# Moving one VectorE step of a unit function by half an item in 18 items, and 27 sums from GpSimd to VectorE

## The chip, the cores and the metric

The kernel runs on one core of a Trainium2 chip, in one launch. The metric is the device time of that launch in microseconds; several runs are given by their median. TensorE (PE) does the matmuls into PSUM, VectorE (DVE), ScalarE (ACT) and GpSimd (POOL) the element-wise work, and SyncE (SP) issues nearly all transfers. Each engine works its instructions off in the order in which they stand in its queue.

## What is computed

Three layers in a row, in float32. Only their core matters here:

```python
# 1: linear attention with decay, 4 batches x 8 heads, 768 steps of 48
state = alpha[:, :, t, :, None] * state + np.einsum('bhd,bhe->bhde', k[:, :, t], v[:, :, t])
y[:, :, t] = np.einsum('bhd,bhde->bhe', q[:, :, t], state)
# 2: x is 3072 x 384 from here on; w_in 384 x 2048, w_out 2048 x 384
h = x @ w_in
g = np.where(h > 0.0, h, alpha * (np.exp(np.minimum(h, 0.0)) - 1.0))
x = g @ w_out
# 3: four experts of 1024 hidden units, weighed by normalised probabilities
for e in range(E):
    h = np.maximum(x @ w1[e], 0.0)
    out += p[:, e:e + 1] * (h @ w2[e])
```

## The kernel before

The 3072 tokens are worked in six chunks of 512 (128 positions of four batches). To keep float32 accuracy with fast matmuls, each operand is split into a high part (a ScalarE copy with rounding, "cast") and a low part (a subtraction, `value - high`), and each product is three matmuls: high by high, high by low, low by high.

**Attention** (units of 128 positions of one batch, four to a chunk). A unit's steps are `scores` (two PSUM banks a, L252), `ktrans` (transposes of k into a bank h, L273), `prep0` to `prep2` for the next unit (running products P on VectorE, L207; Ln and Exp on ScalarE, L215 to L217; products nt, raw on VectorE, L230 to L242, the last of them q times P), `yout_t` and `state` (L309, L316, L343), the masked scores sm (VectorE, L260), the copy yt (ScalarE, L324), a way out to memory and back into another layout (x0d, then xr), and `xtrans`, which splits xr into the second layer's x (L377, L378). After `state`, VectorE adds tmp and st (L353, L355). The first chunk's units run ahead of the main loop.

**Second layer.** The main loop of `run` goes over 96 items. An item is one block f of 128 hidden units of one chunk c. The order is chunk 0 with f = 0 to 7, chunk 1 with all 16, chunk 0 with f = 8 to 15, then chunks 2 to 5. In item i TensorE runs `first` (nine matmuls h = w x, L425, into one of three banks h0 to h2, which the transposes of `ktrans` use in turn with them) and `second` of item i - 2 (nine matmuls t += w g, L450). Between them the unit function and its split are made:

- `elu(h)`: ScalarE e = relu(-h) (L434), e = exp(-e) (L435), then VectorE h = max(e - 1, h) in place in PSUM (L436);
- `parts(h)`: ScalarE g high = copy of h (L441) at once; VectorE g low = h - g high (L442), returned as `low` and run later.

In the loop, `self.queue` holds deferred steps; `flush` runs them, twice an item; `slots` holds the attention steps of the next chunk and the weights' conversions by half item; `post` holds steps at an item's end. The first FS = 8 items split h right after `elu`; the others at the item's end, with the low part first in the next flush. Weights of the second layer come as 64-bit words in a buffer ring of two (wraw, L394) and are converted by ScalarE (cv, L408) and three VectorE steps on bits (L78, L81, L84), then split (w_W, L377, L378). The conversions f = 3 to 15 lie in items 0 to 15. When a part of a chunk ends, three ScalarE copies x1raw (L963) empty the banks t.

**Third layer.** From the end of the second layer on, three blocks at a time are multiplied by a scheme that needs sums of x blocks: for the first pair of chunks `prep_x0` makes 12 sums xs (`sum_x`, L567) and splits 15 blocks into tiles xc (`split`), spread over the items 81 to 94, beside the preparation of the third layer's weights (`prep_w`, tiles wc and wh). Before, the sums and the low parts of xc are on GpSimd.

What sets the order: TensorE, ScalarE, VectorE and GpSimd run in the order in which the code is written (`manual_schedule`). Only the transfers on SyncE are placed by a scheduler, which may put them in another order when the code moves.

## Time and profile before

| what | value |
|---|---|
| median of three runs | 1289.72 us (1289.24 to 1292.94) |
| profiled execution | 1294.53 us, span 1292.7 us |
| mean granted clock of TensorE | 0.985 of full speed |
| second layer with the rest of the attention | about 39 to 552 us |
| third layer | about 552 us to the end |

The profile lists, for each instruction or group, its start, its duration and, in brackets, how long its engine stood idle before it and which engine, tile and line ended that wait. L numbers are lines of the kernel before; in the changed kernel lines from 66 on are one higher, and those behind L436 move with the edits. The rows that are used stand in a section below.

### The profile page before, as it was taken

What the parts mean: (1) busy time and instruction counts of PE and PEld (TensorE: products, weight loads), DVE (VectorE), ACT (ScalarE), POOL (GpSimd) and SP (SyncE); (2) the same over time, 40 slices, a digit from 0 to 9 for tenths busy, and PEclk for the clock granted to TensorE, in tenths of its full rate; (3) what the DMA queues carried; (4) which work ended last, traced back from release to release, by engine and by line L of the source; (5) the groups of instructions that cost most, each with busy time, mean ns of one, the idle gap of its engine ahead of it and who ended that gap; (6) DMA issues with size and microseconds to landing.
All of it is one profiled execution on the core that took longest, in us unless ns stands there. A gap on an engine that the chain in (4) does not pass through costs nothing.

```text
span 1292.7 us, 17676 instructions
## 1 busy us (share of the span) xinstructions
PE 1248.4 (97%) x6453; PEld 1015.9 (79%) x6457; DVE 892.4 (69%) x1513; ACT 588.2 (46%) x1076; POOL 522.2 (40%) x405
## 2 busy tenths in 40 slices
PE   8687999999999999999999999999999999999997
PEld 6566788788888888778888888788888878888886
DVE  8976766787777867766757666666667576657664
ACT  5555655566666656633334341434333233233241
POOL 0000000000000004738679774777779475456562
PEclk8789999999999999999999999999999999999999
DMA  6543325566565647744646468755555775435232
GB/s 227 196 159 114 106 64 170 187 241 221 209 220 183 238 166 250 264 183 158 235 145 231 176 233 338 249 216 195 204 191 203 266 291 183 173 106 204 98 114 72
DMA packets 71823, 248.28 MB, mean 192 GB/s; under 512 B 6712, under 2 KB 38296, under 8 KB 62384
## 3 DMA queue, kind: packets, MB, share of 16 engines
q1 hardware_dynamic: 70720, 241.56, 52.6%
q10 hardware_dynamic: 1008, 5.51, 1.1%
q8 instruction: 53, 0.87, 0.3%
q14 instruction: 42, 0.34, 0.1%
HBM read 182.89 MB, written 64.14 MB: 191 GB/s over the span
## 4 chain that ended last, share of the span: by engine, by line
PE 82%; DVE 7%; ACT 4%; DMA 3%; issue 2%; POOL 1%; SPq 0%; ACTq 0%; DVEq 0%; POOLq 0%
PE h L729 24%; PE t L776 14%; PE t L450 12%; PE h L425 11%; PE a L776 10%; PE h L776 5%; PE a L252 2%; PE a L309 1%; PE a L316 1%; DMA wraw<-in_wm_dram 1%; PE h L273 1%; DMA xr<-x0d 1%; DVE cv L81 1%; DVE h L436 1%; DVE wh L378 1%
## 5 line engine op out<-in xcount | busy, mean ns | idle before, releaser
L749 DVE TENSOR_TENSOR u<-h,u 128x512 f32<-128x512 f32 x258 | 177.6, 688 | 87.4 <-PE h L729 86.4
L707 POOL TENSOR_TENSOR g_W<-c,g_W 128x512 fp32r<-128x512 f32 x128 | 164.6, 1301 | 156.4 <-ACT c L705 127.7
L450 PE MATMUL t<-g,w_W 128*128 128x512 f32 x864 | 218.9, 397 | 8.1 <-ACT x1raw L963 3.3
L729 PE MATMUL h<-xc_Q,wa 128*128 128x512 f32 x780 | 218.8, 390 | 2.8 <-DVE c L749 2.2
L425 PE MATMUL h<-x,w_W 128*128 128x512 f32 x864 | 216.9, 395 | 3.4 <-ACT x L377 2.8
L567 POOL TENSOR_TENSOR xs<-xr 128x512 f32<-128x512 f32 x8 | 12.4, 1568 | 494.5 <-DVE wc L478 494.5
L704 ACT ACTIVATE g_W<-c 128x512 fp32r<-128x512 f32 x128 | 80.2, 627 | 265.9 <-DVE c L749 149.5
L450 PEld LDWEIGHTS t<-g,w_W 128*128 128x128 f32 x864 | 162.1, 190 | 45.9 <-DVE g L442 5.6
L425 PEld LDWEIGHTS h<-x,w_W 128*128 128x128 f32 x864 | 161.8, 189 | 39.2 <-ACT x L377 3.6
L729 PEld LDWEIGHTS h<-xc_Q,wa 128*128 128x128 f32 x780 | 145.9, 188 | 35.0 <-DVE c L749 2.6
L776 PE MATMUL t<-g_W,wb 128*128 128x512 f32 x576 | 157.6, 389 | 0.0
L436 DVE SCALAR_TENSOR_TENSOR h<-e,h 128x512 f32<-128x512 f32 x96 | 66.6, 694 | 97.4 <-ACT e L435 97.1
L776 PEld LDWEIGHTS t<-g_W,wb 128*128 128x128 f32 x576 | 108.1, 188 | 22.5
L705 ACT ACTIVATE c<-c 128x512 f32<-128x512 f32 x192 | 121.4, 633 | 7.5 <-POOL g_X L707 0.4
L749 DVE TENSOR_TENSOR c<-u,h 128x512 f32<-128x512 f32 x123 | 84.1, 686 | 46.4 <-PE h L729 42.0
L743 DVE COPY u<-h 128x512 f32<-128x512 f32 x99 | 67.9, 690 | 64.1 <-PE h L729 63.8
L729 PE MATMUL h<-xc_W,wa 128*128 128x512 f32 x390 | 110.0, 391 | 0.8 <-DVE c L749 0.7
L707 POOL TENSOR_TENSOR g_X<-c,g_X 128x512 fp32r<-128x512 f32 x64 | 82.0, 1298 | 67.9 <-ACT c L705 64.5
L776 PE MATMUL a<-g_W,wb 128*128 128x512 f32 x384 | 108.4, 389 | 0.0
L704 ACT ACTIVATE g_X<-c 128x512 fp32r<-128x512 f32 x64 | 40.1, 626 | 131.4 <-DVE c L749 73.3
L729 PEld LDWEIGHTS h<-xc_W,wa 128*128 128x128 f32 x390 | 72.8, 188 | 17.7 <-DVE c L749 1.6
L442 DVE TENSOR_TENSOR g<-h,g 128x512 fp32r<-128x512 f32 x96 | 65.8, 685 | 27.4 <-ACT g L441 27.2
(139 smaller groups left out, 1943.1 us busy)
## 6 DMA issues: line engine op xcount, KB each, us to landing
wa<-wad SPq DMA_DIRECT2D x33, 1536.0 KB, 6.5
wb<-wbd SPq DMA_DIRECT2D x30, 1536.0 KB, 7.2
raw<-in_att_dram SPq DMA_DIRECT2D x22, 960.0 KB, 4.9
wad<-wh SPq DMA_DIRECT2D x44, 384.0 KB, 2.7
wbd<-wh SPq DMA_DIRECT2D x43, 384.0 KB, 4.4
xcd<-xh SPq DMA_DIRECT2D x30, 512.0 KB, 3.2
wraw<-in_wm_dram SPq DMA_DIRECT2D x16, 768.0 KB, 4.4
wraw<-in_we_dram SPq DMA_DIRECT2D x20, 576.0 KB, 4.7
```

What stands on the lines that cost most here:

```text
L252: nc.tensor.matmul(ps[j][:, a * C:(a + 1) * C], raw[r, K0 + a * C:K0 + (a + 1) * C], raw[r, Q0 + a * C:Q0 + (a + 1) * C], start=True, stop ...
L425: nc.tensor.matmul(h[:, 0:n], w[:, wl, fi, k * 128:(k + 1) * 128], x[:, xl, k, n0:n0 + n], start=(k == 0 and i == 0), stop=(k == KD - 1 an ...
L436: nc.vector.scalar_tensor_tensor(out=h, in0=e, scalar=-1.0, in1=h, op0=ALU.add, op1=ALU.max)
L442: return g, lambda: nc.vector.tensor_tensor(out=g[:, 1], in0=h, in1=g[:, 0].bitcast(F32), op=ALU.subtract)
L450: nc.tensor.matmul(self.xa[k][:, 0:n], w[:, wl, fi, DM + k * 128:DM + (k + 1) * 128], g[:, gl, 0:n], start=(first and i == 0), stop=(last ...
L704: nc.scalar.activation(out=g[:, n, 0], in_=v, func=AF.Relu)
L705: nc.scalar.activation(out=v, in_=v, func=AF.Relu)
L707: lambda: nc.gpsimd.tensor_tensor(out=g[:, n, 1], in0=v, in1=g[:, n, 0].bitcast(F32), op=ALU.subtract)
L729: nc.tensor.matmul(b, w[:, wl], x[:, xl], start=(j == 0), stop=(j == 2))
L743: nc.vector.tensor_copy(out, b)
L749: (nc.vector if "b" in (a0, a1) or dst == "S5" else nc.gpsimd).tensor_tensor(out=out, in0=val(a0, b), in1=val(a1, b), op=ALU.add if op == ...
L776: nc.tensor.matmul(oa[m, d], wt[:, f, wl, d * 128:(d + 1) * 128], G[m][:, f, gl], start=first, stop=last)
```

## The change

A constant WIDE = 18 is added. `elu` no longer issues its VectorE step but returns it. For items 0 to 17 that step (L436) is issued at the item's end, behind the second flush, `second`, the half item's slots and `post`; the high copy of g (L441) follows in the next item behind its `first`, and the low part (L442) behind that item's first flush and first slots. From item 18 on the order is what it was. In `prep_x0` the sums and the low parts name VectorE and no longer GpSimd.

```diff
--- before.py
+++ after.py
@@ -63,6 +63,7 @@
 )
 ORDER = [p for p, _ in STEPS]
 WSLOT = {p: i for i, p in enumerate((7, 11, 1, 6, 4, 2, 13, 12, 10, 3, 8, 14, 0, 9, 5))}
+WIDE = 18
 WPREP = (28, 92)
 
 
@@ -433,7 +434,7 @@
         e = self.ep.tile([128, 512], F32, tag="e", name="e")
         nc.scalar.activation(out=e, in_=h, func=AF.Relu, scale=-1.0)
         nc.scalar.activation(out=e, in_=e, func=AF.Exp, scale=-1.0)
-        nc.vector.scalar_tensor_tensor(out=h, in0=e, scalar=-1.0, in1=h, op0=ALU.add, op1=ALU.max)
+        return lambda: nc.vector.scalar_tensor_tensor(out=h, in0=e, scalar=-1.0, in1=h, op0=ALU.add, op1=ALU.max)
 
     def parts(self, h):
         nc = self.nc
@@ -586,13 +587,13 @@
 
         def base(p):
             s[p] = tmp[:, len(s)]
-            self.sum_x(nc.gpsimd, s[p], p, x, s)
+            self.sum_x(nc.vector, s[p], p, x, s)
 
         def summ(p):
             if p not in s and len(XSUM[p]) > 1:
                 v[p] = tmp[:, 2 + sn[0] % 4]
                 sn[0] += 1
-                self.sum_x(nc.gpsimd, v[p], p, x, s)
+                self.sum_x(nc.vector, v[p], p, x, s)
 
         def one(p):
             i = ORDER.index(p)
@@ -600,7 +601,7 @@
                 tiles.append(self.xc_tile())
             t, i = tiles[i // 3], i % 3
             y = s[p] if p in s else v[p] if p in v else x[XSUM[p][0]]
-            self.split(t[:, i, 0], t[:, i, 1], y, nc.gpsimd)
+            self.split(t[:, i, 0], t[:, i, 1], y)
 
         self.xc[0] = tiles
         st = [[(loads, (0,)), (loads, (1,)), (loads, (2,))]]
@@ -974,14 +975,21 @@
         order = tc.manual_schedule(engines={e.PE, e.Activation, e.DVE, e.Pool})
         order.__enter__()
         self.queue = []
+
+        gone = None
         for i in range(n1):
-            h = first(items[i])
+            h, late = first(items[i]), i < WIDE
+            if gone:
+                gs[items[i - 1]], low = self.parts(gone)
             self.flush()
             for s in slots.pop((i, 0), []):
                 do(s)
-            self.elu(h)
-            if i < FS:
-                gs[items[i]], low = self.parts(h)
+            if gone:
+                low()
+                gone = None
+            unit = self.elu(h)
+            if not late:
+                unit()
             self.flush()
             if i >= LA:
                 second(items[i - LA])
@@ -989,9 +997,12 @@
                 do(s)
             for f, a in post.pop(i, []):
                 f(*a)
-            if i >= FS:
+            if late:
+                unit()
+                gone = h
+            else:
                 gs[items[i]], low = self.parts(h)
-            self.queue.insert(0, low)
+                self.queue.insert(0, low)
         while self.queue:
             self.flush()
         assert not slots and not post and not loads
```

TensorE's order is the same in both kernels. Three places show what moves on the others.

VectorE, items 0 and 1 (h_537 is the h of item 0; cv and wraw belong to weight conversions, sm to the masked scores, g is the low part). Before:

```order
L436 SCALAR_TENSOR_TENSOR h_537<-e,h_537 128x512
L78 TENSOR_SCALAR cv<-cv 128x768
L81 SCALAR_TENSOR_TENSOR cv<-wraw_482,cv 128x768
L84 SCALAR_TENSOR_TENSOR cv<-wraw_482,cv 128x768
L260 TENSOR_TENSOR sm<-a_549,mask 128x512
L260 TENSOR_TENSOR sm<-a_550,mask 128x512
L442 TENSOR_TENSOR g<-h_537,g 128x512
L78 TENSOR_SCALAR cv<-cv 128x768
L81 SCALAR_TENSOR_TENSOR cv<-wraw_530,cv 128x768
L84 SCALAR_TENSOR_TENSOR cv<-wraw_530,cv 128x768
```

Now:

```order
L79 TENSOR_SCALAR cv<-cv 128x768
L82 SCALAR_TENSOR_TENSOR cv<-wraw_482,cv 128x768
L85 SCALAR_TENSOR_TENSOR cv<-wraw_482,cv 128x768
L261 TENSOR_TENSOR sm<-a_549,mask 128x512
L261 TENSOR_TENSOR sm<-a_550,mask 128x512
L437 SCALAR_TENSOR_TENSOR h_537<-e,h_537 128x512
L79 TENSOR_SCALAR cv<-cv 128x768
L82 SCALAR_TENSOR_TENSOR cv<-wraw_530,cv 128x768
L85 SCALAR_TENSOR_TENSOR cv<-wraw_530,cv 128x768
...
L443 TENSOR_TENSOR g<-h_537,g 128x512
```

L436 (now L437) of item 0 went from ahead of the first bits to behind sm, and g's low part from behind sm to behind the bits and the preparation (nt, raw) that follow.

ScalarE, items 0 and 1 (e is the exponential, g the high part, kn and yt attention copies, h_594 or h_592 the h of item 1). Before:

```order
L434 ACTIVATE e<-h_537 128x512
L435 ACTIVATE e<-e 128x512
L441 CAST g<-h_537 128x512
...
L408 ACTIVATE cv<-wraw_530 128x768
L434 ACTIVATE e<-h_594 128x512
L435 ACTIVATE e<-e 128x512
L441 CAST g<-h_594 128x512
L377 CAST w_W_525<-cv 128x768
L324 COPY yt<-a_614 112x512
```

Now:

```order
L435 ACTIVATE e<-h_537 128x512
L436 ACTIVATE e<-e 128x512
L280 COPY kn<-h_559 128x512
...
L409 ACTIVATE cv<-wraw_530 128x768
L442 CAST g<-h_537 128x512
L435 ACTIVATE e<-h_592 128x512
L436 ACTIVATE e<-e 128x512
L378 CAST w_W_525<-cv 128x768
L325 COPY yt<-a_613 112x512
```

The copy of g of item 0 went behind the attention's steps, and no copy of g of item 1 stands ahead of yt any more.

VectorE, items 11 and 12 (h_1198 or h_1196 is the h of item 11; w_W_1133 or w_W_1132 a weight's low part). Before:

```order
L436 SCALAR_TENSOR_TENSOR h_1198<-e,h_1198 128x512
L442 TENSOR_TENSOR g<-h_1198,g 128x512
L378 TENSOR_TENSOR w_W_1133<-cv,w_W_1133 128x768
L78 TENSOR_SCALAR cv<-cv 128x768
L81 SCALAR_TENSOR_TENSOR cv<-wraw_1180,cv 128x768
L84 SCALAR_TENSOR_TENSOR cv<-wraw_1180,cv 128x768
L436 SCALAR_TENSOR_TENSOR h_1229<-e,h_1229 128x512
```

Now:

```order
L437 SCALAR_TENSOR_TENSOR h_1196<-e,h_1196 128x512
L379 TENSOR_TENSOR w_W_1132<-cv,w_W_1132 128x768
L79 TENSOR_SCALAR cv<-cv 128x768
L82 SCALAR_TENSOR_TENSOR cv<-wraw_1179,cv 128x768
L85 SCALAR_TENSOR_TENSOR cv<-wraw_1179,cv 128x768
L443 TENSOR_TENSOR g<-h_1196,g 128x512
L437 SCALAR_TENSOR_TENSOR h_1227<-e,h_1227 128x512
L79 TENSOR_SCALAR cv<-cv 128x768
```

The low part of g of item 11 stood ahead of the weight's low part and its next bits, and now stands behind them.

## Rows read from the trace of the kernel before

**Rows 1.** The page's part 1: busy time of an engine, share of the span, instructions.

```profile
PE 1248.4 (97%) x6453; PEld 1015.9 (79%) x6457; DVE 892.4 (69%) x1513; ACT 588.2 (46%) x1076; POOL 522.2 (40%) x405
```

**Rows 2.** Windows, TensorE alone: length, busy time, granted clock, DMA share, GB/s.

```profile
39.00:166.00 127.00, 102.86 (x604) 0.89 0.41 138
...
300.00:552.00 252.00, 251.44 (x1466) 1.00 0.63 219
```

**Rows 3.** Windows: busy time of PE, PEld, DVE, ACT, POOL, then granted clock.

```profile
46.00:112.00 66.00, 49.05 (x361) 39.79 (x361) 50.03 (x84) 34.37 (x65) 0.00 (x0) 0.82 0.45 149
78.00:81.00 3.00, 2.71 (x18) 2.48 (x19) 2.97 (x8) 0.46 (x1) 0.00 (x0) 0.50 0.65 190
```

**Rows 4.** Waits, 39 to 170 us: who waited for whom; total, times, longest.

```profile
ACT g L441 <- DVE h L436: 28.4, 17, 4.8
DVE h L436 <- ACT e L435: 21.8, 8, 6.0
...
ACT cv L408 <- DMA wraw<-in_wm_dram: 4.2, 2, 3.1
```

**Rows 5.** Timeline of TensorE, 39 to 166 us: rows with the long waits.

```profile
51.09 1.97 PE L309 MATMUL a<-raw,st 48*64 48x128 f32 x16 [5.40 <-DVE sm L260]
59.71 2.08 PE L252 MATMUL a<-raw 48*128 48x128 f32 x16 [3.95 <-ACT yt L324]
...
75.03 0.49 PE L252 MATMUL a<-raw 48*128 48x128 f32 x2 [1.50 <-ACT yt L324]
78.29 2.07 PE L252 MATMUL a<-raw 48*128 48x128 f32 x14 [2.78 <-DVE tmp L353]
92.19 1.18 PE L252 MATMUL a<-raw 48*128 48x128 f32 x16 [0.85 <-ACT yt L324]
...
111.74 0.50 PE L425 MATMUL h<-x,w_W 128*128 128x512 f32 x1 [2.78 <-ACT x L377]
...
126.24 2.14 PE L450 MATMUL t<-g,w_W 128*128 128x512 f32 x8 [3.31 <-ACT x1raw L963]
...
155.15 3.68 PE L450 MATMUL t<-g,w_W 128*128 128x512 f32 x8 [2.11 <-DVE g L442]
```

**Rows 6.** Timeline of ScalarE and VectorE in item 0.

```profile
45.22 0.89 ACT L408 ACTIVATE cv<-wraw 128x768 f32<-128x768 f32 x1 [1.20 <-DMA wraw<-in_wm_dram]
...
47.29 0.69 DVE L436 SCALAR_TENSOR_TENSOR h<-e,h 128x512 f32<-128x512 f32 x1 [2.27 <-ACT e L435]
47.89 0.55 DVE L78 TENSOR_SCALAR cv<-cv 128x768 int32<-128x768 int32 x1
...
50.35 1.28 DVE L260 TENSOR_TENSOR sm<-a,mask 128x512 f32<-128x512 f32 x2
```

**Rows 7.** Timeline of ScalarE and VectorE in item 1.

```profile
57.13 0.69 DVE L436 SCALAR_TENSOR_TENSOR h<-e,h 128x512 f32<-128x512 f32 x1
...
57.85 0.59 ACT L441 CAST g<-h 128x512 fp32r<-128x512 f32 x1 [4.79 <-DVE h L436]
...
59.07 0.59 ACT L324 COPY yt<-a 112x512 f32<-112x512 f32 x1
```

**Rows 8.** Timeline of items 2 and 3.

```profile
70.36 0.69 DVE L436 SCALAR_TENSOR_TENSOR h<-e,h 128x512 f32<-128x512 f32 x1 [5.50 <-ACT e L435]
...
81.06 3.48 PE L450 MATMUL t<-g,w_W 128*128 128x512 f32 x9
```

**Rows 9.** Timeline of VectorE, the low part of item 11.

```profile
138.13 0.69 DVE L442 TENSOR_TENSOR g<-h,g 128x512 fp32r<-128x512 f32 x1 [3.25 <-ACT g L441]
```

**Rows 10.** Groups by line and form: 496 to 546, 440 to 490, page; count, busy, mean ns.

```profile
L378 DVE TENSOR_TENSOR wh<-wraw,wh 128x384 fp32r<-128x384 f32 x5 | 6.1, 1214 | 0.0
...
L378 DVE TENSOR_TENSOR wh<-wraw,wh 128x384 fp32r<-128x384 f32 x5 | 2.8, 552 | 0.0
...
L567 POOL TENSOR_TENSOR xs<-xr 128x512 f32<-128x512 f32 x8 | 12.4, 1568 | 494.5 <-DVE wc L478 494.5
```

**Rows 11.** Chain that ended last, around 300 us: start, length, work.

```profile
300.53 2.04 PE h L425 x9
```

## The prediction

> **What bounds the kernel now.** I read the share of busy time first. TensorE is busy 97% of the span [rows 1], so only time in which it stands still, or runs at the lower of its clock levels, can be won. Two windows then say where that is [rows 2]: from 300 to 552 us it works 251.44 of 252, but from 39 to 166, the stretch of the 18 items that the change touches, only 102.86 of 127. About 24 us stand open there, and the granted clock is 0.89. From 46 to 112 us VectorE has 50.03 us of work in 66, at a clock of 0.82 [rows 3]. So in that stretch neither engine is full: the time goes into handing over.
>
> The list of waits names the hand-overs [rows 4]: ScalarE waits 28.4 us for the unit function's last step (h, VectorE, L436) before it may copy the high part of g, and VectorE waits 21.8 us for the exponential (e, ScalarE) before it may run that step. Both queues run in order, so what stands behind these two waits too, and TensorE waits for that. Its eight long waits [rows 5] are 5.40 + 3.95 + 1.50 + 2.78 + 0.85 + 2.78 + 3.31 + 2.11 = 22.7 us. None names h or e; they name what is queued behind: the masked scores (sm), the copy yt, the state's sum (tmp), the copy of x, the copies x1raw, and g's low part.
>
> **The change, part one: the unit function spread.** No instruction is added or taken away here; in items 0 to 17 three move. L436 goes behind the half-item's other VectorE work, g's high copy into the next item, g's low part behind that item's first steps. TensorE's order is as before. I follow the lead that TensorE gains over the old trace, wait by wait.
>
> First wait, 5.40 for sm. Before, VectorE stood 2.27 us for e, ran L436 at 47.29, then the weight bits from 47.89, then sm from 50.35 [rows 6]. Now the bits need only the copy cv (45.22 + 0.89 = 46.11), so all of it starts 1.74 earlier. Lead 1.7; 3.65 us of wait stay, since the bits and sm (2.46 us, then the first of two 0.64) still lie ahead.
>
> Second wait, 3.95 for yt. Before, ScalarE stood 4.79 us for L436, which ran last behind a whole preparation step, at 57.13 [rows 7], so yt came at 59.07. In the new ScalarE order no copy waiting for that L436 stands ahead of yt. The next late thing is the last step of the preparation, q times P, which the same matmuls read. It ended where L436 began, 57.13; ahead of it stand as many steps as before (L436 in place of the low part, 0.60 each), so 57.13 - 1.74 = 55.4. The copy cv before its bits now comes behind two ScalarE steps of another order; I allow 0.4 for that and take 55.8 against 59.71. Lead 3.9. Bounds: 2 if cv is late by one more 2.46 us step, 5 if TensorE runs at once after its state matmuls.
>
> Third and fourth, 1.50 and 2.78 (yt, then tmp). Behind them lies VectorE's wait of 5.50 us for e at 70.36 [rows 8]: the copy of x waited for its transfer, e stood behind that copy. The transfer starts with yt, now some 5 us earlier, and L436 now comes after the preparation. Carried on step by step with the same durations VectorE has no gap here, yt ends at 70.6 and tmp's first read at 71.4, while TensorE is ready at 69.7: 1.7 us of wait stay, 2.6 go. Lead 6.5.
>
> The clock of this place. TensorE ran at 0.50 of full speed, its 1.2 GHz level, at 78 to 81 us [rows 3], after those two waits: 14 score matmuls took 2.07 us where 16 at 92.19 took 1.18 [rows 5], and nine of L450 3.48 us [rows 8] where eight at 126.24 took 2.14, that is 2.4 for nine. With the waits down to 1.7 I take full speed: 0.9 + 1.1 and about half a microsecond of the transposes between them, 2.5 in all. Lead 9.0. If the clock falls all the same, 2.5 less. That it falls is rival (e).
>
> Fifth and sixth, 0.85 for yt and 2.78 for the copy of x at 111.74. By the same steps 0.4 and 1.4 stay: the last x transfer starts when yt is out, and its way through memory does not get shorter. Lead 10.8. A floor speaks for not taking more: VectorE's own 50 us of work from 46 on [rows 3] leave at most 16 of the 66.
>
> Seventh, 3.31 for x1raw: these three copies stand on ScalarE behind a high copy that waits for L436, and L436 now stands behind the weight bits, as x1raw's buffer did before. About 0.2 goes. Lead 11.
>
> Then a new wait. At 138.13 VectorE stood 3.25 us for g's high copy and ran the low part before the next weight's bits [rows 9]. In the new order the bits (2.46) stand ahead of this low part, as the third piece of order above shows. TensorE has some 0.3 to spare there, so 2.2 us are lost. Lead 8.8. Last, 2.11 for g at 155.15: in the old order one low part stood behind bits that came late; now it comes behind an L436 that is ready, and I find it 0.5 us ahead of need. The wait goes, and the low clock behind it (eight matmuls in 3.68 against 2.14, 1.5 us) with it; 0.3 us of new wait appear an item later. Lead 8.8 + 2.1 + 1.5 - 0.3 = 12.1.
>
> From there to 552 us TensorE has no gap to speak of, and all loads are placed by item, so the lead is kept: 12 us.
>
> **Part two: the first pair's sums.** 12 sums and 15 low parts leave GpSimd, where a sum takes 1568 ns, for VectorE [rows 10]. At 0.60 each, start to start (47.29 to 47.89), they add 27 x 0.60 = 16.2 us to VectorE between 496 and 546. Against it, five of VectorE's 128x384 steps with two inputs took 1214 ns while GpSimd ran and 552 before [rows 10]: 3.3 us come back there, and if a dozen other steps of the kind in this stretch lose as much, 11 in all. Net 5 us of VectorE work over 13 items, 0.4 each, and TensorE hardly waits in this stretch (0.6 us in 252) [rows 2]. A low part is made some 3.4 us after its item's first matmuls end and needed 8.2 after, two items of 4.1 (2.04 for nine matmuls, twice) [rows 11]. Cost to TensorE: 0, bounds -0.5 (those small waits go) and +4 (nothing comes back and the slack is used up). The Trainium skill (SBUF — State Buffer, SBUF: two separate sides) has the two engines lock each other out of a port pair for a whole instruction. The trace agrees in kind, 552 against 1214 ns, but shows 0.66 us and not GpSimd's whole 1568 ns; by the page more would come back on VectorE, and the sum would be the 0.5 us of the lower bound better.
>
> **The sum.** The profiled execution took 1294.53 us, 1.8 over its span of 1292.7, and lies 4.8 above the median 1289.72. Against its own time: 1294.5 - 12 = 1282.5. Against the median 1277.7. The longer execution may hold more of the low clock than the median one; against that, I counted nothing for the low clock before 66 us. I set these off. Forecast **1277.5**.
>
> **The rivals.**
> (a) *Weight bits ahead of low parts.* Four conversions between items 10 and 15 now have bits ahead of a low part; I found room for all but one. If it is missing each time, 3 x 2.2 = 6.6 us more are lost: 1284. For it: ScalarE waited for a weight load up to 3.1 us here [rows 4], and VectorE now stands behind that ahead of g. Against: other loads than that longest come in time.
> (b) *Loads set the pace.* If weights and the attention's data cannot come sooner, only the first three gains of order stay, some 4 us: 1285.5. Against it: in all of 39 to 170 us ScalarE waited twice for a weight, 4.2 us [rows 4].
> (c) *Banks: slower.* h has three PSUM banks, and a bank is free only when the low part has read it. That read now comes half an item later, while the transposes of the first six items take turns in the same banks. At 4.1 us an item a bank is wanted again 10.2 us after its matmuls end (three items less nine matmuls) [rows 11]. The chain is two ScalarE steps (1.3), L436 and two copies (1.9), and what stands between, up to two sets of bits (4.9) and a weight's low part: some 9. If it passes 10.2 by 1.5 us in each of the items 6 to 17, 12 x 1.5 = 18 us are lost against 12 won: 1296. Against: in my steps the tightest bank is free 0.5 us early, and the first six items have the gaps.
> (d) *Part two stalls TensorE* by its whole bound, 4 us: 1281.5.
> (e) *The clock falls again.* Low stretches followed the waits of 1.50 and 2.78 and the one of 2.11, and none followed the single 3.31 [rows 3, 5]. If 1.7 us of wait are enough at 71, and 2.2 at 127, the 2.5 does not come back and 1.5 are paid anew: 1281.5. The Trainium skill (TensorE: Matmul & The Clock Gate, What's actually happening) has a low clock as the default, which activity alone lifts; by it waits that are shortened but not gone can keep it low. The rows bear it out so far as each low stretch stands behind a wait.
> (f) *More than I took:* the clock stays high from 49 us on and the waits 3.65 and 3.31 shrink: 8 us more, 1269.5.
>
> **How the numbers follow.** Forecast 0.46, (a) 0.15, (b) 0.10, (c) 0.08, (d) 0.08, (e) 0.07, (f) 0.06. The range takes in (a), (d) and (e) and goes up to (b)'s near side and down by most of (f): 1271 to 1285. A measurement of this kernel can tell about 0.3%, 3.9 us, from no change: bounds 1285.8 and 1293.6. (b) lies at the edge and is split: faster 0.46 + 0.15 + 0.08 + 0.07 + 0.06 and half of (b), 0.87; within 0.05; slower 0.08.
>
> **What would show it.** Right: sm for the second stretch near 48.6 and its matmuls near 49.3; score matmuls of the next unit near 56; ScalarE's waits for L436 well below 28 us; first matmuls on the second chunk near 101; a wait of about 2 us for g near 127; none of 2.11 later; VectorE without 1.2 us steps from 485 to 535, GpSimd idle until the third layer. Wrong: TensorE waits of over 1 us at L425 for a low part (banks), waits for weight transfers in VectorE's or ScalarE's list, or new waits for g between 485 and 535.

## The result and the profile after

The changed kernel took 1279.63 us (median of four runs, 1274.29 to 1281.86) against 1291.33 for the kernel before on the same chip: a ratio of 0.9899 [0.9855, 0.9943], 11.7 us less. Measured once more beside other kernels it took 1277.85 against 1292.55, ratio 0.9895 [0.9879, 0.9911], 14.7 us less by the medians. The forecast was 1277.5, or 12 us.

The page's part 1 (busy time of an engine, share of the span, instructions) answers [rows 1]. TensorE is busy 98% now. The same matmuls took it 4 us less, with less of them at the low clock (mean granted clock 0.989 after 0.985); VectorE has 4.6 us more work, GpSimd 37.6 us less.

```profile
PE 1244.5 (98%) x6453; PEld 1014.6 (79%) x6457; DVE 897.0 (70%) x1540; ACT 587.5 (46%) x1076; POOL 484.6 (38%) x378
```

Two stretches as windows (length, then busy time of PE, PEld, DVE, ACT, POOL, granted clock, DMA share, GB/s) answer [rows 2, 3]. From 46 to 101 us VectorE has about the work that it had before in 66 us.

```profile
39.00:153.00 114.00, 102.31 (x616) 81.52 (x615) 97.06 (x152) 68.50 (x119) 0.00 (x0) 0.92 0.46 155
46.00:101.00 55.00, 46.83 (x362) 37.85 (x360) 49.25 (x83) 32.41 (x62) 0.00 (x0) 0.88 0.54 182
```

TensorE's waits in that stretch (start, duration, operation, and in brackets the idle time and what ended it) answer [rows 5]. "issue" in the second row is a wait that the profile names no releaser for; q times P, which these matmuls read, is the VectorE step L243 that ended just before (54.30 + 0.68, shown below).

```profile
48.70 1.09 PE L310 MATMUL a<-raw,st 48*64 48x128 f32 x16 [2.45 <-DVE sm L261]
...
55.09 2.89 PE L253 MATMUL a<-raw 48*128 48x128 f32 x16 [3.11 <-issue]
...
69.60 0.48 PE L253 MATMUL a<-raw 48*128 48x128 f32 x2 [0.96 <-ACT yt L325]
70.48 1.83 PE L253 MATMUL a<-raw 48*128 48x128 f32 x14 [0.39 <-DVE tmp L354]
...
84.18 1.16 PE L253 MATMUL a<-raw 48*128 48x128 f32 x14 [1.12 <-DVE tmp L354]
...
114.65 3.81 PE L451 MATMUL t<-g,w_W 128*128 128x512 f32 x9 [2.72 <-ACT x1raw L964]
...
129.67 2.11 PE L451 MATMUL t<-g,w_W 128*128 128x512 f32 x8 [0.66 <-DVE g L443]
```

They add up to 11.4 us, where the eight of before made 22.7. The wait of 2.11 for g and the one for the first copy of x on chunk 1 are gone; the one for x1raw is still there.

The list of waits (total, times, longest), 39 to 160 us, answers [rows 4]. ScalarE waits for the unit function's last step as long as before, 28.5 us. But VectorE's wait for the exponential, 21.8 us before, is down to 2.7 (6.0 in the second trace of the change).

```profile
ACT g L442 <- DVE h L437: 28.5, 14, 4.5
...
DVE g L443 <- ACT g L442: 3.3, 5, 0.7
DVE h L437 <- ACT e L436: 2.7, 5, 1.0
```

VectorE in items 0 and 1 (timeline) answers [rows 6]: sm directly behind the weight bits, L437 behind sm, and the low part (L443) only behind the next bits and the preparation step.

```profile
47.09 0.96 DVE L85 SCALAR_TENSOR_TENSOR cv<-wraw,cv 128x768 int32<-128x768 int32 x1
47.96 1.28 DVE L261 TENSOR_TENSOR sm<-a,mask 128x512 f32<-128x512 f32 x2
49.16 0.68 DVE L437 SCALAR_TENSOR_TENSOR h<-e,h 128x512 f32<-128x512 f32 x1
49.91 0.56 DVE L79 TENSOR_SCALAR cv<-cv 128x768 int32<-128x768 int32 x1
...
54.30 0.68 DVE L243 TENSOR_TENSOR raw<-raw,P 128x512 f32<-128x512 f32 x1
54.91 0.68 DVE L443 TENSOR_TENSOR g<-h,g 128x512 fp32r<-128x512 f32 x1
```

Part two, by groups (shapes, count, busy time, mean ns) from 483 to 539 us, answers [rows 10]: the two-input steps of 128x384 take 549 ns, where five took 1214.

```profile
L379 DVE TENSOR_TENSOR wh<-wraw,wh 128x384 fp32r<-128x384 f32 x5 | 2.7, 549 | 0.0
```

**The lead, read across all kernels.** TensorE's order is the same in nearly all kernels of this study, so each matmul's start can be set against its start in the trace of before. The table gives this lead in us, less the lead at the first scores of the main loop (41.86 in the trace of before), so that what differs in the start-up is taken out. A column is the start of a TensorE group in the old trace: 51.09, 59.71 and 75.03 are the three first waits of [rows 5], 84.37 the first h matmuls behind the low clock, 111.74 the first on chunk 1, 126.24 those that wait for x1raw, 130.49 the next second matmuls, 150.61 just ahead of the wait of 2.11, 170.63 behind it all.

| kernel | 51.09 | 59.71 | 75.03 | 84.37 | 111.74 | 126.24 | 130.49 | 150.61 | 170.63 |
|---|---|---|---|---|---|---|---|---|---|
| the change | 2.95 | 5.18 | 5.99 | 9.23 | 11.26 | 12.15 | 10.59 | 11.39 | 15.15 |
| the change, again | 2.96 | 5.20 | 6.01 | 10.81 | 12.53 | 13.43 | 11.84 | 13.05 | 16.80 |
| part one | 2.95 | 5.13 | 5.95 | 10.76 | 10.32 | 11.22 | 11.25 | 9.08 | 13.10 |
| part two | 1.28 | 1.28 | 1.26 | 0.67 | 1.26 | 1.24 | 1.26 | 1.35 | 1.34 |
| items 0 to 7 only | 2.96 | 5.18 | 6.00 | 10.81 | 10.34 | 10.60 | 7.92 | 9.65 | 10.02 |
| items 8 to 17 only | 1.03 | 1.03 | 0.97 | 0.70 | 2.73 | 3.35 | 1.76 | 2.65 | 6.39 |
| low part first | 1.81 | 2.86 | 3.52 | 4.21 | 6.44 | 4.43 | 4.44 | 3.54 | 4.95 |
| split late | 1.28 | 3.67 | 1.12 | 0.47 | 0.72 | -2.47 | -2.43 | -2.37 | -2.38 |
| low part behind, L437 early | 1.14 | 4.13 | 1.72 | 1.64 | 3.70 | 3.96 | 2.39 | 3.02 | 6.66 |
| low part first in 8 to 17 | 2.97 | 5.14 | 5.96 | 10.77 | 10.39 | 11.29 | 11.30 | 10.09 | 11.51 |
| WIDE = 80 | 2.98 | 5.20 | 6.02 | 10.83 | 10.81 | 11.70 | 10.36 | 11.41 | 15.11 |
| dummies | 2.97 | 5.20 | 6.02 | 9.27 | 11.24 | 12.13 | 12.16 | 13.37 | 17.12 |
| dummies and WIDE = 80 | 2.97 | 5.21 | 6.03 | 10.84 | 10.67 | 11.57 | 11.61 | 13.15 | 16.91 |

The row of part two, whose order is the old one up to 496 us, shows what must be taken off: 1.3 us (the three other kernels whose L436 stands in its old place there have 1.0 to 1.3 at the first wait). The profiled execution of before had lost them at its first wait. There cv waited 1.20 us for a weight transfer ahead of the exponential [rows 6], and TensorE waited 5.40; in the kernel with part two alone that wait was 4.13:

```profile
51.71 1.97 PE L309 MATMUL a<-raw,st 48*64 48x128 f32 x16 [4.13 <-DVE sm L260]
```

So the change's own lead over the old order ends at 15.15 - 1.3 = 13.9 us in one execution and 15.5 in the other.

### The profile page after: what moved, and what is told of

Same layout as the page of the kernel before. It is cut to its first block, busy times and chain, and to the rows that moved or that the text cites. A ratio compares the mean times of both kernels' runs of the same rounds, so it can differ in the third digit from the quotient of the medians.

```text
span 1276.3 us, 17673 instructions
## 1 busy us (share of the span) xinstructions
PE 1244.5 (98%) x6453; PEld 1014.6 (79%) x6457; DVE 897.0 (70%) x1540; ACT 587.5 (46%) x1076; POOL 484.6 (38%) x378
## 4 chain that ended last, share of the span: by engine, by line
PE 85%; DVE 6%; ACT 3%; issue 2%; DMA 2%; POOL 1%; SPq 0%; ACTq 0%; DVEq 0%; POOLq 0%
PE h L730 24%; PE t L777 14%; PE t L451 13%; PE h L426 13%; PE a L777 10%; PE h L777 5%; PE a L253 1%; PE a L310 1%; PE a L317 1%; DMA raw<-in_att_dram 1%; PE h L274 1%; DVE P L208 1%; DVE cv L82 1%; ACT cv L409 1%; DVE h L437 1%
## 5 line engine op out<-in xcount | busy, mean ns | idle before, releaser
L437 DVE SCALAR_TENSOR_TENSOR h<-e,h 128x512 f32<-128x512 f32 x96 | 66.5, 692 | 70.2 <-ACT e L436 69.9
L777 PEld LDWEIGHTS a<-g_W,wb 128*128 128x128 f32 x384 | 72.1, 188 | 15.0
L443 DVE TENSOR_TENSOR g<-h,g 128x512 fp32r<-128x512 f32 x96 | 65.8, 686 | 25.2 <-ACT g L442 24.9
```

The source lines that it names most:

```text
L437: return lambda: nc.vector.scalar_tensor_tensor(out=h, in0=e, scalar=-1.0, in1=h, op0=ALU.add, op1=ALU.max)
L443: return g, lambda: nc.vector.tensor_tensor(out=g[:, 1], in0=h, in1=g[:, 0].bitcast(F32), op=ALU.subtract)
L777: nc.tensor.matmul(oa[m, d], wt[:, f, wl, d * 128:(d + 1) * 128], G[m][:, f, gl], start=first, stop=last)
```

## The experiments

**Part one alone.**

```diff
-            self.sum_x(nc.vector, s[p], p, x, s)
+            self.sum_x(nc.gpsimd, s[p], p, x, s)
...
-            self.split(t[:, i, 0], t[:, i, 1], y)
+            self.split(t[:, i, 0], t[:, i, 1], y, nc.gpsimd)
```

> The unit function spread in items 0 to 17, sums and low parts of the first pair still on GpSimd. In the two profiled executions TensorE's lead of the new order over the old is 14.6 us at 230 us of the old trace and stays there up to 527, then grows to 16.1 by 541. Theory (hand-overs): part one alone gives the 14.6, and the last 1.5 is part two's. In the trace the lead is 14 to 15 at 552; in the median 1279 to 1282, 1 to 2 us above the whole change. Rival (part two costs or gives more): if this kernel is faster than the whole change by 2 us or more, part two stalls TensorE; if slower by over 3, part two carries a share that I had put at nothing.

Measured 1281.15 against 1292.12, ratio 0.9913 [0.9893, 0.9933]: 11.0 us of the gain. In the trace TensorE's lead stays level from 525 to 541 us. It is 13.1 - 1.3 = 11.8 at 170, and 12.3 us counted from the span's start at 552, where I had expected 14 to 15. The wait near 129 is the predicted one, in size too:

```profile
115.08 2.34 PE L451 MATMUL t<-g,w_W 128*128 128x512 f32 x9 [2.72 <-ACT x1raw L964]
129.89 2.77 PE L451 MATMUL t<-g,w_W 128*128 128x512 f32 x8 [2.04 <-DVE g L443]
```

**Part two alone.** The same lines the other way, in the kernel before.

> The kernel before with only the 12 sums and 15 low parts on VectorE. Theory: TensorE's order up to 496 us is as before with all eight long waits, and from 496 on two waits for g's low part (0.22 and 0.27) and the small losses beside them go: 0.5 to 1.5 us faster than before, 1289 to 1291; VectorE's 128x384 steps with two inputs all take about 0.55 us. Rival: the 16.2 us added to VectorE bring new waits for g, up to 4 us slower than before, 1294.

Measured 1291.75 against 1292.12, ratio 0.9995 [0.9983, 1.0007]: no difference that can be measured, and none of the 4 us that the rival has. In the trace 1.5 us are won between 525 and 541 us (the lead goes from -0.56 to 0.91, and likewise from 14.59 to 16.06 in the change, both counted from the span's start); in this trace they go again at the third layer's start, with the low clock that the last section shows. The kernel before shows where; the two listed waits, each behind the first matmul of a group, cost about 0.3 us more than their length. From 533.40 to 535.96 are 2.56 us and from 538.00 to 540.64 are 2.64, where a group without a wait takes 2.04 to the start of the next [rows 11]: 0.52 lost for a wait of 0.22, and 0.60 for one of 0.27. The wait of 0.66 in the change cost 0.96 in the same count (128.62 to 131.62).

```profile
533.40 0.39 PE L450 MATMUL t<-g,w_W 128*128 128x512 f32 x1
534.01 2.11 PE L450 MATMUL t<-g,w_W 128*128 128x512 f32 x8 [0.22 <-DVE g L442]
535.96 2.20 PE L425 MATMUL h<-x,w_W 128*128 128x512 f32 x9
538.00 0.39 PE L450 MATMUL t<-g,w_W 128*128 128x512 f32 x1
538.66 2.14 PE L450 MATMUL t<-g,w_W 128*128 128x512 f32 x8 [0.27 <-DVE g L442]
540.64 2.21 PE L425 MATMUL h<-x,w_W 128*128 128x512 f32 x9
```

**Items 0 to 7 only**, without part two.

```diff
-WIDE = 18
+WIDE = 8
```

> Part one with WIDE = 8, part two left out: only the items that run beside the attention's steps are spread. Theory (hand-overs): the lead is 11 at the first matmuls on chunk 1, and nothing is gained behind it: 1280 to 1283, with the wait of 2.11 for g's low part and the half clock behind it still there near 144. Rival (loads set the pace): the lead gained up to 112 us shrinks to 4 or less by 170 us, since the weights come when they come: 1286 to 1288.

Measured 1282.73, ratio 0.9926 [0.9912, 0.9941]: 9.4 us by the medians. The lead does not shrink behind the attention, as it would if loads set the pace. The wait for g that the late items lose in the change stands here, with the low clock behind it (eight matmuls in 3.63):

```profile
142.98 3.63 PE L451 MATMUL t<-g,w_W 128*128 128x512 f32 x8 [1.79 <-DVE g L443]
```

**Items 8 to 17 only**, without part two.

```diff
-            h, late = first(items[i]), i < WIDE
+            h, late = first(items[i]), FS <= i < WIDE
...
+            if i < FS:
+                gs[items[i]], low = self.parts(h)
             self.flush()
...
             else:
-                gs[items[i]], low = self.parts(h)
+                if i >= FS:
+                    gs[items[i]], low = self.parts(h)
                 self.queue.insert(0, low)
```

> Items 0 to 7 as before, only items 8 to 17 spread, part two left out. Theory: no lead up to 112 us; then up to 1.5 lost, and 4 won where the wait of 2.11 stood with its half clock: 2.5 to 4 faster than before, 1287 to 1288.5. Rival 1: the late items gain only because the first eight bring the weights' conversions forward: no change, 1290 to 1291.5. Rival 2 (weight bits ahead of low parts): each of the conversions between items 10 and 15 costs up to 2.2, slower than before, 1293.

Measured 1289.48, ratio 0.9985 [0.9971, 0.9998]: 2.6 us by the medians, 1.9 by the ratio, where I had expected 2.5 to 4. The trace has 6.4 - 1.0 = 5.4 of lead, more than the times; why is open. In the times the parts add up: by the ratios 9.6 and 1.9 make 11.5, and part one measured 11.2.

**The low part first.** In the spread items the low part follows its high copy at once; L437 keeps its late place.

```diff
                 gs[items[i - 1]], low = self.parts(gone)
+                low()
+                gone = None
...
-            if gone:
-                low()
-                gone = None
```

> The whole change, but in items 0 to 17 g's low part is issued right behind its high copy, ahead of the item's first deferred steps and its weight bits. Theory (low part behind bits, rival a's mechanism once): TensorE's wait for g's low part near 129 us, 0.66 in the changed kernel and 2.04 in the kernel with part one alone, goes; in items 0 to 7 VectorE now stands about 1 us for the high copy ahead of the masked scores and of the state's sum, and 1 to 3 us of lead are lost there. In all 1279 to 1283. Rival: the early place costs nothing, since VectorE has room, and the kernel is 1 to 2 us faster than the changed one, 1277.5 to 1278.5.

Measured 1289.87 against 1292.48, ratio 0.9982 [0.9969, 0.9995]. Both expectations were far off: they had 1 to 3 us of loss against the change, or a gain of 1 to 2, and the ratios show a loss of about 11. VectorE's waits show it (39 to 160 us):

```profile
DVE g L443 <- ACT g L442: 20.7, 17, 4.5
...
DVE h L437 <- ACT e L436: 0.7, 1, 0.7
```

It no longer stands for the exponential, but now for the high copy, as long as it stood for the other before. The end of the attention shows why, at the place where the most is lost, a lead of 6.44 falling to 1.63 within 5 us (timeline of the three engines):

```profile
103.01 0.51 ACT L378 CAST x<-xr 128x384 fp32r<-128x384 f32 x1 [3.46 <-DMA xr<-x0d]
103.43 0.58 ACT L442 CAST g<-h 128x512 fp32r<-128x512 f32 x1
...
104.04 0.69 DVE L443 TENSOR_TENSOR g<-h,g 128x512 fp32r<-128x512 f32 x1 [4.54 <-ACT g L442]
...
107.71 2.89 PE L426 MATMUL h<-x,w_W 128*128 128x512 f32 x8 [3.63 <-DVE x L379]
```

ScalarE waits for a transfer, the high copy waits behind that, VectorE's low part behind the copy, and behind the low part the weight bits and x, which TensorE needs. With the low part behind the bits, VectorE does these meanwhile.

**Split late.** In the kernel before, items 0 to 7 are split at the item's end; L436 stays where it was.

```diff
-            if i < FS:
-                gs[items[i]], low = self.parts(h)
...
-            if i >= FS:
-                gs[items[i]], low = self.parts(h)
+            gs[items[i]], low = self.parts(h)
```

> The kernel before, in which items 0 to 7 split h at the item's end like the others; the unit function's last step stays where it was, and GpSimd keeps its sums. Theory: VectorE still stands for the exponential in each item ahead of the weight bits and sm, so the first wait of 5.40 stays whole; ScalarE's copy of g no longer stands ahead of yt, so that of the second wait and behind it some goes: 3 to 5 us faster than before, 1286.5 to 1289. Rival 1: ScalarE's wait was all of it; then it gains as much as WIDE = 8 did, 9.4: 1282.5. Rival 2: VectorE's wait was all of it: no change, 1291.

Measured 1297.12, ratio 1.0033 [1.0020, 1.0045]: slower, which none of the three expectations had. At the second wait the copy's new place wins 2.4 us (lead 3.67 against 1.28), but by 75.03 that is gone. VectorE stands for both now:

```profile
DVE h L436 <- ACT e L435: 18.7, 7, 5.7
DVE g L442 <- ACT g L441: 12.3, 5, 4.6
```

So moving the high copy to a later place by itself loses some 4 us.

**WIDE = 80**, with part two: 62 more items spread.

> The whole change with WIDE = 80 and not 18: 62 more items, with TensorE at work without a gap, are spread. Theory: the chain from the h matmuls' end to the low part's end stays under the 10.2 us after which its bank is wanted again, and a low part comes in time for the second matmuls two items on: no TensorE wait over 0.5 us at the h matmuls, 1278 to 1281. Rival (banks, c): 1.5 us are lost in each spread item, 62 x 1.5 = 93: 1372. Rival in between: only the items with weight conversions of the third layer (28 to 79) lose some tenths each, 1285 to 1300.

Measured 1278.92, ratio 0.9895 [0.9875, 0.9914], as the change. TensorE's waits from 155 to 540 us hold one for a bank of h, of 0.2 us:

```profile
PE t L451 <- ACT x1raw L964: 1.2, 1, 1.2
PE h L426 <- DVE g L443: 0.2, 1, 0.2
```

The banks are no limit at this pace, with more than four times as many spread items.

**Dummies.** 26 matmuls that nobody reads, of 128x512, in three of the waits: 8 ahead of the wait for sm, 10 ahead of the scores behind it, 8 ahead of the second matmuls that wait for x1raw.

```diff
+    def dummy(self, tag, n):
+        ps = self.bank(tag)
+        for i in range(n):
+            self.nc.tensor.matmul(ps, self.w1[0][:, 0, 0, 0:128], self.x0[0][:, 0, 0], start=True, stop=True)
...
+        if u == (1, 1):
+            self.dummy("t0", 10)
...
+        if u == (1, 0):
+            self.dummy("t0", 8)
...
+            if i == FS + LA:
+                self.dummy(self.ab[0], 8)
             if i >= LA:
```

> The whole change, with 26 matmuls whose result nobody reads put into three of TensorE's waits: 8 ahead of the 2.45 for sm, 10 ahead of the 3.11 for q times P, 8 ahead of the 2.72 for x1raw (each 128x512, about 0.23 us at full speed, so that the waits cover them). Theory (the low clock behind a wait comes from standing still): the 16 score matmuls behind the second wait take about 1.2 us, not 2.89, and the nine behind x1raw 2.2, not 3.81; of these 3.3 us part is given back to the next waits, above all that for g's low part near 129, which grows from 0.66 to about 2: 1 to 2 us faster than the change, 1277.5 to 1278.5. Rival: the low clock comes at those places whatever TensorE does, and nothing changes, 1279.5; or the dummies delay what stands behind them, slower by up to 2.

Measured 1275.63, ratio 0.9878 [0.9856, 0.9899], the fastest so far. The rows with the waits, and the nine h matmuls behind the second (line numbers 7 to 9 higher):

```profile
54.58 0.46 PE L260 MATMUL a<-raw 48*128 48x128 f32 x2 [1.31 <-issue]
55.40 1.16 PE L260 MATMUL a<-raw 48*128 48x128 f32 x14 [0.36 <-DVE tmp L363]
...
57.25 3.53 PE L435 MATMUL h<-x,w_W 128*128 128x512 f32 x9
...
114.18 2.34 PE L460 MATMUL t<-g,w_W 128*128 128x512 f32 x9 [0.93 <-ACT x1raw L973]
...
127.20 2.11 PE L460 MATMUL t<-g,w_W 128*128 128x512 f32 x8 [0.25 <-DVE g L452]
```

At the scores the dummies did not keep the clock up. The 14 score matmuls took 1.16 us, but the nine h matmuls behind them 3.53 (3.18 in the change), at a granted clock of 0.64 from 57 to 61 us; and in the other trace with these dummies, that with WIDE = 80 too, the 14 themselves were slow:

```profile
55.27 1.91 PE L260 MATMUL a<-raw 48*128 48x128 f32 x14 [0.36 <-DVE tmp L363]
```

The 0.9 us that the h matmuls start earlier are given back by the next wait (lead 6.02 at 75.03, as all the others). At x1raw the nine matmuls took 2.34 and 2.33 us in the two traces with dummies, and the 1.5 us are kept (lead 12.13, then 12.16, where the change has 12.15, then 10.59); the wait for g did not grow as I had expected. But two of the six traces without dummies and with a wait of about that length were as quick there, and one of them, part one, lost the time again at the wait near 129. Behind it all the lead, less 1.3, is 15.8 and 15.6 us with the dummies, and 13.9, 15.5 and 13.8 without (the change twice, WIDE = 80). Against the change itself the dummies are 2.2 to 4.0 us quicker by the medians of its two measurements, but 0.17 to 0.21% by the ratios, whose intervals overlap: a gain that the traces and the times suggest and do not show.

**The low part behind, L437 early.** The change, with L437 right behind the exponential as in the kernel before.

```diff
-            if not late:
-                unit()
+            unit()
             self.flush()
...
             if late:
-                unit()
                 gone = h
```

> The whole change, but the unit function's last VectorE step stands where it stood before, right behind the exponential, ahead of the second flush; g's high copy and its low part stay at their new places in the next item. Theory now (after the kernel with the low part first lost some 9 of the 12 us): it is the low part's place behind the weight bits that frees VectorE, and the step L436's place matters little: 1280 to 1283. Rival (the prediction's): VectorE standing for the exponential ahead of the bits and sm is the larger part, the first wait is above 5 again, and half the gain or more is gone: 1285 to 1290.

Measured 1286.56 against 1292.55, ratio 0.9961 [0.9949, 0.9973]: half of the gain is gone, the rival's case. TensorE's first wait is back (timeline), with 4.27 us, where the rival has over 5, and VectorE stands 17.8 us for the exponential again:

```profile
49.92 1.97 PE L310 MATMUL a<-raw,st 48*64 48x128 f32 x16 [4.27 <-DVE sm L261]
```

VectorE's row in the list of waits, 39 to 160 us:

```profile
DVE h L437 <- ACT e L436: 17.8, 7, 4.9
```

**The low part first in items 8 to 17 only.**

```diff
                 gs[items[i - 1]], low = self.parts(gone)
+                if i > FS:
+                    low()
+                    gone = None
```

> The whole change, with g's low part right behind its high copy in items 8 to 17 only; in items 0 to 7 it stays behind the bits. Theory: the lead up to 105 us is that of the change (11), so the low-first kernel's loss lay in items 0 to 7; behind it the wait for g's low part near 129 (0.66 to 2.04) goes, but each item pays 0.2 to 0.5 for a low part just too late, as in the low-first kernel at 137 to 154, 2.5 us in all: 1279 to 1282. Rival: the late items lose as much as the early ones, 1284 or more.

Measured 1282.04, ratio 0.9915 [0.9898, 0.9931]. That is at the upper end of what I expected (1279 to 1282). The lead at 126 us, 11.3, is that of part one (11.2), one to two us under the change's, the wait near 129 shrinks to 0.23, and then each item pays: the lead falls from 11.30 to 10.09 between 130.49 and 150.61, and only 1.4 follow where the change wins 3.8. So the low part first costs 2.6 us by the ratios in the late items, and most of its loss of 11 lay in the first eight.

**WIDE = 80 and the dummies together**, and **the change again**.

> The 26 unread matmuls and WIDE = 80 together. Theory: the two do not touch the same waits; WIDE = 80 brought nothing beyond scatter, so this is as the dummies alone, 1275 to 1277. Rival: WIDE = 80 takes the small waits of 1.3 and 1.2 us near 240 away, and they add up: 1273 to 1274.

> The changed kernel once more, beside the others on one chip, so that they are compared with it and not only with the kernel before: 1278 to 1281. If the dummies' kernel stands 2 us or more below it, the half clock behind its waits was on the path.

Measured 1275.60, ratio 0.9873 [0.9854, 0.9891], and 1277.85, ratio 0.9895 [0.9879, 0.9911], on the same chip. The first is the fastest kernel of the study, by a little; WIDE = 80 brings it nothing that can be told from scatter, and against the change it is 2.2 us less, with intervals that overlap.

## Why the prediction held, step by step

**First and second wait.** Predicted leads 1.7 and 3.9; the table gives 2.95 - 1.28 = 1.7 and 5.18 - 1.28 = 3.9. These steps rested on the order alone, and they came out to a tenth in every kernel that has the change's order in items 0 to 7.

**Third and fourth, and the clock there.** Predicted 6.5, and 9.0 with the clock back. Measured at 84.37, less what part two's row has there (0.67): 8.6 in the change, 10.1 in its second trace. The waits left are 1.35 as against 1.7, and the clock came back only in part in the first trace (14 score matmuls in 1.83 us) and wholly in the second (1.16). Size right, the two traces 1.6 us apart.

**Fifth, sixth, seventh.** Predicted 10.8 and 11.0; measured 10.0 and 10.9 (11.26 and 12.15, less 1.3), 11.3 and 12.2 the second time. The first matmuls on chunk 1 start at 101.04 (about 101 predicted), and the wait for x1raw has become 2.72 where I kept 3.1. What I left out stands behind that wait: nine second matmuls took 3.81 us, at the low clock, against 2.34 with the dummies. That is 1.5 us lost, the second part of rival (e)'s price, but at a place that I had cleared, because none had followed the 3.31 of before.

**The new wait.** Predicted 2.2 behind the weight bits near 127. It stands there with 0.66, 0.26 and 0.42 in three traces and 2.04 in part one. The mechanism is the predicted one, and what sets its size is a transfer (ScalarE and VectorE in the change):

```profile
125.54 0.89 ACT L409 ACTIVATE cv<-wraw 128x768 f32<-128x768 f32 x1 [2.89 <-DMA wraw<-in_wm_dram]
...
126.46 0.56 DVE L79 TENSOR_SCALAR cv<-cv 128x768 int32<-128x768 int32 x1 [2.83 <-ACT cv L409]
...
128.93 0.68 DVE L443 TENSOR_TENSOR g<-h,g 128x512 fp32r<-128x512 f32 x1
```

The low part waits behind bits that wait for a weight. Counted from the first scores, cv starts 83.1 us on in the change, 83.8 in part one and 81.1 with the dummies. So the term was taken at its upper end. Rival (a), 6.6 us more of the kind, did not come.

**The wait of 2.11.** Predicted 2.1 + 1.5 - 0.3 = 3.3. Between 150.61 and 170.63 the change wins 15.15 - 11.39 = 3.8, the kernel with items 0 to 7 alone 0.4. That these are the late items is shown by those two kernels and by items 8 to 17 alone (2.65 to 6.39).

**The end of the sum.** Predicted 12.1; 13.9 and 15.5 in the two traces of the change, 11.8 for part one. The terms that missed (1.5 of low clock lost behind x1raw, up to 1.9 of the new wait not lost, 1.6 more won between 141 and 151, where the kernel before had waits of 0.41 and 0.23 for g that I had not listed) do not cancel: the lead came out 1.8 and 3.4 us above the forecast in the two traces of the change. By the medians, 11.7 and 14.7. That the forecast of 1277.5 lies so close to the measured times is in part luck: its base, 1289.72 from three runs, is 1.6 to 2.8 us below the kernel before in all later medians (1291.33 to 1292.55), and this offset the lead that I had taken too small.

**Part two.** Predicted 0, bounds -0.5 and +4; measured -0.4 us [-2.2, +0.9], and 1.5 won in the trace. VectorE's busy time in 56 us ahead of the third layer rose from 41.45 to 46.40, 5 us (4.6 over the whole kernel), as I had netted it; TensorE has no gap there. The window of the kernel before (columns as above) and, under it, the one of the change:

```profile
496.00:552.00 56.00, 55.44 (x243) 44.87 (x242) 41.45 (x62) 38.66 (x78) 37.50 (x27) 1.00 0.71 258
```

```profile
483.00:539.00 56.00, 56.00 (x249) 46.37 (x248) 46.40 (x90) 38.85 (x76) 0.00 (x0) 1.00 0.77 271
```

The lower bound was too tight: I took the two waits at their listed length. A step that takes 1214 ns beside GpSimd takes 549 ns without it, the same as alone, so all of what a step lost comes back. I had set that mean loss, 0.66 us, against the whole 1568 ns of a GpSimd sum. Single steps of the kernel before show that this was the wrong comparison:

```profile
510.60 1.29 POOL L378 TENSOR_TENSOR xc_Q<-xs,xc_Q 128x512 fp32r<-128x512 f32 x1 [0.64 <-ACT xc_Q L377]
510.65 1.66 DVE L378 TENSOR_TENSOR wh<-wraw,wh 128x384 fp32r<-128x384 f32 x1
```

This VectorE step began 0.05 us behind the GpSimd instruction and ended 0.42 us behind its end: it lost 1.1 us of 1.29. The five steps took 0.67 to 1.66 us, according to where they fell. The Trainium skill (SBUF — State Buffer, SBUF: two separate sides) says that whichever of the two starts first holds the port pair for its whole instruction while the other blocks. The trace agrees: a step that falls into the middle of a GpSimd instruction waits for less than the whole, hence the mean of 0.66 us.

**Why it works.** Here the prediction told half. It put the gain down to the new places of L436 and of g's high copy, and the low part's new place, behind the bits, to the costs. Four kernels tell the two VectorE moves apart. Split late has both steps at their old places and the high copy at its late one; up to 160 us all four have the same order on TensorE and ScalarE, and VectorE's order differs by L436's place alone, by the low part's alone, or by both (VectorE's waits from 39 to 160 us in the traces, leads at 170.63 less 1.3):

| kernel | waits for e | waits for g high | lead |
|---|---|---|---|
| before (high copy early in items 0 to 7) | 21.3 | 5.2 | 0 |
| split late | 18.7 | 12.3 | -3.7 |
| low part first, L437 late | 0.7 | 20.7 | 3.7 |
| low part behind, L437 early | 17.8 | none | 5.4 |
| both (the change) | 2.7 | 3.3 | 13.9 |

The high copy's late place alone costs 3.7 us. From there L437's late place wins 7.4, the low part's 9.1, and both win 17.6: they nearly add up, and the 1.1 left over is less than two traces of the change differ by (1.6). The ratios of the times say much the same: 4.3 lost, then 6.6, 9.3 and some 17.5 won, part two's share in each of the last three. Counted from the kernel before, each of the two seems worth only 4 to 5, since each then also pays for the high copy. An item has two round trips between VectorE and ScalarE. With L437 late and the low part first, part of the wait only changes place: 18.0 us of waiting for the exponential go, and 8.4 more for the high copy come. With the low part behind and L437 early, the wait for the high copy goes and that for the exponential stays, 17.8. My steps had carried the low part at its new place, hence a sum near the measured one; I had only not seen what it was worth. ScalarE's wait for L436, which I wanted "well below 28 us", is 28.5: that sign was wrong. ScalarE can afford to stand there, since sm, yt and the bits no longer stand behind it.

One difference was not tested apart: up to 160 us the scheduler of SyncE swaps three pairs of neighbouring transfers in the change, against the kernel before. The kernel with the low part first has two of the three swaps, one other, and little of the gain; that with L437 early has the old order.

**The range.** It reached from 1271 to 1285, and the medians of the change, 1279.63 and 1277.85, lie near its middle. Of the rivals, (b) falls with the lead of items 0 to 7 that stays, (c) with WIDE = 80, (d) with part two alone; of (e) one stretch and, in one trace, part of another came. (a) did not come, nor did (f): the score matmuls behind the second wait took 2.89 us, at the low clock.

## What to carry to other kernels

Where two in-order engines pass a tile back and forth inside an item, find all the trips and move the steps of all of them: here one of three moves alone lost 3.7 us, and with the two others, worth 7 and 9, the lead was 13.9. Judge each move from a kernel that has the others as well, not only from the one before, where the cost of the first hides the gain of the next. Put the step that answers the other engine behind work that needs no answer, and check which transfer that work waits for, since the answer then waits for it too. Count a short wait behind the first matmul of a group at its listed length and about 0.3 us more, and look whether the clock stays up behind it.

## What the hardware showed unexpectedly

**The same wait, two clocks.** The wait for x1raw of 2.72 to 2.75 us, with the same work ahead of it, was followed by nine matmuls in 3.81, 3.91 and 3.67 us in three traces (the change, again, WIDE = 80) and in 2.34 and 2.35 in two others (part one, low part first in 8 to 17); with items 8 to 17 only, 2.76 us of wait were followed by 3.17. With eight unread matmuls in it, it was 2.34 and 2.33. Up to there the change and part one are the same program. A window at that place (columns as above), first of the change:

```profile
114.00:118.00 4.00, 3.35 (x9) 2.64 (x10) 1.72 (x3) 3.54 (x8) 0.00 (x0) 0.64 0.41 162
```

The same place in the kernel with the low part first in items 8 to 17:

```profile
115.00:118.00 3.00, 2.91 (x13) 2.39 (x14) 0.87 (x3) 2.55 (x6) 0.00 (x0) 1.00 0.41 159
```

A wait of 2.16 at the third layer's start does the same: three matmuls behind it took 0.96 in the change (timeline)

```profile
553.82 0.96 PE L730 MATMUL h<-xc_Q,wa 128*128 128x512 f32 x3 [2.16 <-DVE c L750]
```

and 1.47 in the kernel with part one alone:

```profile
557.55 1.47 PE L730 MATMUL h<-xc_Q,wa 128*128 128x512 f32 x3 [2.16 <-DVE c L750]
```

So one trace without a low clock behind a wait does not clear that wait. The Trainium skill (TensorE: Matmul & The Clock Gate, What's actually happening) says that the count of slow matmuls at a kernel's start differs from run to run of one kernel. In the middle of this one two traces of the change differ in the same way: the 14 score matmuls of its third and fourth wait took 1.83 us in one and 1.16 in the other.

**The start.** Up to the first scores of the main loop the executions differ by 4.2 us (leads from -2.02 to 2.20), whatever the order behind it; behind that point the first three waits repeat to 0.1 us. Most of the scatter between the runs of one kernel, 1274 to 1282, may lie there; that was not measured apart.
